# Attention in front of two MLPs: small DMAs, scaling, products with V and weight steps at other steps of the loop

## The chip, the cores and the metric

The kernel runs on one core of a Trainium2 chip. The metric is the device time of one execution in microseconds; the median of three runs of the kernel before is 731.0 us (729.5 to 731.06).

## What is computed

The reference pools neighbouring queries in pairs, does softmax attention, and puts the result through two MLPs:

```python
q_pool = q.reshape(B, H, S // 2, 2, D).mean(axis=3)          # B=2, H=8, S=1152, D=64
scores = np.matmul(q_pool, k.transpose(0, 1, 3, 2)) / np.sqrt(D)
scores = scores - np.max(scores, axis=-1, keepdims=True)
attn = np.exp(scores)
attn = attn / (np.sum(attn, axis=-1, keepdims=True) + 1e-09)
x = np.matmul(attn, v)                                       # -> 1152 tokens x 512
h = x @ w_in;  x = (h * np.tanh(softplus(h))) @ w_out        # 512 -> 2048 -> 512
h = x @ w_in2; y = elu(h) @ w_out2                           # 512 -> 2048 -> 512
```

All arrays that the host hands over are float64 for the MLP weights (the kernel reads them as words of 64 bits) and float32 for the rest.

## The kernel before, in words

**Pairs, units, steps.** Attention takes two heads at a time: 8 pairs `n` of heads, each with 576 pooled queries and 1152 keys. A pair has two units `c`: the first 256 queries and the other 320. A unit has 9 steps `kt`, one for each 128 keys, so a pair has 18 steps and the loop runs over steps `s` from 0 to 143 (then a tail). At each step PE computes the scores of 128 keys with both heads into one PSUM bank pair (`qk`, lines 309 and 311; keys and queries are split into high and low parts, so three products, and a fourth subtracts each query's maximum, which lies in the row tile `top`), and ACT takes the exponential into `pt` (line 317).

**Around this, by unit.** POOL adds up part of the exponentials (`add`, line 330). PE multiplies them with V (`av`, line 382, tile C) and sums them over keys (`total`, line 340, tile T). ACT copies the sums out (`spill`, line 355); they go to DRAM and come back in another layout (lines 357 and 360). DVE inverts them (`invert`, lines 365 and 366); the reciprocals go to DRAM (line 368) and come back broadcast over partitions as `rb` (line 372). DVE multiplies C with `rb` (`scale`, line 406), and ACT and DVE write the high and low part of the tokens that the MLPs read (`token_high`, `token_low`).

**Around this, for a pair ahead.** q, k and V of later pairs are loaded (`load_q`, `load_k`, `load_v`), q is pooled and both are split (`pool_q`, `high_*`, `low_*`). The maximum of each query needs all scores ahead of time: in 14 steps `e` PE computes scores of the next pair with high parts alone (`peak_mm`, tile M, lines 255 and 261, the latter for the 64 queries left over, the rest block) and DVE takes their maxima (`peak`, lines 269 to 273). After `e` = 5 and `e` = 13 `top` negates the maxima (lines 281, 283), sends them to DRAM (line 287) and fetches them back as rows (lines 292, 297).

**Weights.** MLP weights come as float64 words and are turned into a high and a low part in steps: `read` (a DMA, line 99), `rebias` (ACT, 111), `clamp` (POOL, 115), `shift` and `words` (DVE, 120, 125, 126), `high` (ACT, 134), `rest` (DVE, 137). During attention one piece of 512 KB begins in each pair, at step 12; each piece counts its steps (`age`), and the ages decide when its next operation is emitted.

**What sets the order.** There is no planner on the chip: the kernel writes every engine's queue in order. `at(s, e, f)` puts a task into step `s` under a key, and each step emits, in this order: maxima matmuls ("peak"), `qk` and `exp`, products with V and sums ("av"), then "act", "dve", "pool", "sp", then the weight pieces. An engine runs its instructions in the order in which they were emitted, and waits at the first that isn't ready. All DMAs of this part are on SP's queue, and SP too waits at the first DMA whose data isn't ready or whose target isn't free. Scores, maxima scores and sums share one ring of three PSUM tiles (tag S, two banks each); C has two.

Steps below are counted in a pair, so the second unit's step `u0 + 24` is step 33, that is 15 of the next pair:

| task | first unit, before | second unit, before |
|---|---|---|
| `av`, two bursts (5 and 4 of 9) | 11, 15 | 2, 6 |
| `total`; `spill` with both its DMAs | 15; 16 | 6; 7 |
| `invert` with both its DMAs | 2 | 11 |
| `scale`; `token_high`; `token_low` | 6; 7; 9 | 15; 16; 0 |

Maxima of the next pair: steps 5 to 10 and 12 to 17, 0 and 1, each `top` with its DMAs at the step of the last of its maxima. Loads of q and k at step 12, of V at 10. After attention the MLPs run over blocks of 384 tokens (`h_mm`, line 170; `out_mm`, line 617); the scaling of the last pair is done between their first units (`after`).

Of the kernel before, what the change touches and what calls it, by code (L numbers as in the profile page):

```python
# [10 lines left out]
F32 = mybir.dt.float32  # L11
# [10 lines left out]
def tile_pool_attention_mish_elu_mlp(  # L22
# [20 lines left out]
    P = 128  # L43
# [131 lines left out]
    def attention():  # L175
        with ExitStack() as st:
# [102 lines left out]
            def top(n, t0, t1):  # L279
                m, g, row = stat[n], neg[n], tops[n % 2]  # L280
                nc.vector.tensor_reduce(g[:, t0:t1, :], m[:, t0:t1], axis=AX.X, op=ALU.max, negate=True)
                if t1 == NQ:
                    nc.vector.tensor_reduce(g[:, t1, 0:1], m[:, t1, 0:1], axis=AX.X, op=ALU.max, negate=True)
                if t0 == 0:
                    hops[n] = dp.tile([P, NQ + 1, 2], F32, tag="hopm", name="hopm")
                hop, e = hops[n], slice(2 * t0, 2 * t1 + (t1 == NQ))
                nc.sync.dma_start(
                    out=hop.rearrange("p t h -> p (t h)")[:, e], in_=g.rearrange("p t h -> p (t h)")[:, e].bitcast(F32)
                )
# [62 lines left out]
            def spill(n, c):  # L352
                w = cut[c][1] - cut[c][0]
                r = ap.tile([P, 5 * D // 2], F32, tag="sum", name="sum")
                nc.scalar.copy(r[:, :w // 2], sums_.pop((n, c))[:, :w // 2])
                hop = dp.tile([P, w // D], F32, tag=f"hop{c}", name="hop")
                nc.sync.dma_start(out=by_four(hop), in_=r.rearrange("(g p) w -> g p w", p=32)[:, 0, :w // 2])
                pool, bufs = home(n)
                r = tots[n, c] = pool.tile([P, w // D], F32, tag=f"tot{c}", name="tot", bufs=bufs)
                nc.sync.dma_start(out=r, in_=hop)  # L360

            def invert(n, c):
                w = cut[c][1] - cut[c][0]
                r = tots.pop((n, c))
                nc.vector.tensor_scalar(r, r, 1e-9, None, op0=ALU.add)
                nc.vector.reciprocal(r, r)
                hop = dp.tile([P, w // D], F32, tag=f"pop{c}", name="pop")
                nc.sync.dma_start(out=hop, in_=r)
                pool, bufs = home(n)
                rb = rbs[n, c] = pool.tile([P, w], F32, tag=f"rb{c}", name="rb", bufs=bufs)  # L370
                for h in range(2):
                    nc.sync.dma_start(
                        out=rb[half[h]].rearrange("p (z w) -> p z w", z=2),
                        in_=by_four(hop)[2 * h:2 * h + 2].partition_broadcast(D),
                    )
# [47 lines left out]
            last = n_pairs * NS  # L423
            for n in range(n_pairs):
                s0 = n * NS
                if n:
                    at(s0 - 24, "sp", load_q, n)
                    at(s0 - 24, "sp", load_k, n)
# [5 lines left out]
                    at(s0 - 13, "pool", low_q, n, nc.gpsimd)  # L434
                    at(s0 - 11, "pool", low_k, n, nc.gpsimd, slice(0, S // 2))
                    at(s0 - 9, "pool", low_k, n, nc.gpsimd, slice(S // 2, S))
                    at(s0 - 8, "sp", load_v, n)
                    for e in range(6):
                        at(s0 - 13 + e, "peak", peak_mm, n, e)
                        at(s0 - 13 + e, "dve", peak, n, e)  # L440
                    for e in range(6, 14):
                        at(s0 - 6 + e - 6, "peak", peak_mm, n, e)
                        at(s0 - 6 + e - 6, "dve", peak, n, e)
                for c in range(2):
                    u0 = s0 + KT * c
                    for kt in range(KT):
                        at(u0 + kt + 1, "pool", add, n, c, kt)
                        at(u0 + KT + (2 if kt < 5 else 6), "av", av, n, c, kt)
                    t0 = u0 + KT + 6
                    at(t0, "av", total, n, c)  # L450
                    at(t0 + 1, "act", spill, n, c)
                    if n < n_pairs - 1:
                        at(t0 + 5, "dve", invert, n, c)
                        at(t0 + 9, "dve", scale, n, c)
                        at(t0 + 10, "act", token_high, n, c)
                        at(t0 + 12, "dve", token_low, n, c)
                    else:
                        at(t0 + 1, "act", keep, n, c)
                        for u, f in (1 + c, invert), (3 + 3 * c, scale), (3 + 3 * c, token_high), (4 + 3 * c, token_low):
# [26 lines left out]
            low_q(0, nc.gpsimd, c1)  # L486
            for e in range(6, 14):
# [3 lines left out]
                else:  # L491
                    at(e - 10, "peak", peak_mm, 0, e)
                    at(e - 10, "dve", peak, 0, e)
            for s, e in sorted(x for x in todo if x[0] < 0):
# [4 lines left out]
            while s < last or todo or going:  # L499
# [10 lines left out]
                for w in list(going):  # L510
                    w.age += 1
                    if w.age == 4:
                        w.rebias()
                    elif w.age == 5:
                        w.clamp()
                    elif w.age == 7:
                        w.shift()
                    elif w.age == 8:
                        w.words()
                    elif w.age == 9:  # L520
                        w.high()
                    elif w.age == 10:
                        w.rest()
# [238 lines left out]
```

## Time and profile before

| | |
|---|---|
| runs | 731.0 us median (729.5 to 731.06) |
| profiled execution | 730.59 us on the device, span of the instructions 728.8 us |
| mean granted TensorE clock | 0.946 of full |
| busy | PE 668.0 us (92%), DVE 431.4 (59%), ACT 337.8 (46%), POOL 229.6 (32%) |
| DMA | 53.37 MB, 73 GB/s on average |
| attention | to about 316 us; the MLPs fill the rest |

Busy time of PE is that of pipelined matmuls: a matmul's end is modelled, so two in a row can overlap, and a matmul at the lower clock counts as busy for longer. How long a piece of work takes on PE is better read from the starts of successive matmuls. A record "x2" stands for several instructions of the same kind merged into one row.

### The profile page before, as it was taken

To read this page: it belongs to the slowest core of one execution; us is meant where nothing else is said; L and a number is where in the kernel's file an instruction comes from. 1 tells how busy PE (TensorE), PEld (TensorE's weight loads), DVE (VectorE), ACT (ScalarE), POOL (GpSimd) and SP (SyncE) were. 2 spreads that over 40 slices of the span, in tenths; PEclk is the share of its full clock that TensorE was granted. 3 is DMA by queue.
4 is the path that set the end of the run, shared out by engine and by line. 5 is a ranking of instruction groups with operands and counts; after the bars stand their busy time and mean duration, and the time that the engine had idled before them with its cause. 6 is when DMAs were issued, how large, how long until landed. Compare 5 with 4: busy or idle time off the path is not lost.

```text
span 728.8 us, 11613 instructions
## 1 busy us (share of the span) xinstructions
PE 668.0 (92%) x4616; PEld 559.9 (77%) x4616; DVE 431.4 (59%) x700; ACT 337.8 (46%) x680; POOL 229.6 (32%) x213
## 2 busy tenths in 40 slices
PE   4988887888789788979999999999999999999997
PEld 2655555555556555659999999999999999999996
DVE  5555444445454554136745656677698778897453
ACT  2553333435253433444444344444566665675442
POOL 3766364547455263611110123223331101110000
PEclk9999798898969798998999999999999999999999
DMA  3131304040311312133313222222222212320111
GB/s 111 52 127 34 113 9 136 9 137 9 110 36 39 100 23 58 48 95 125 116 58 116 86 62 88 83 87 87 65 80 85 87 61 60 115 87 1 44 44 44
DMA packets 47175, 53.37 MB, mean 73 GB/s; under 512 B 18640, under 2 KB 38032, under 8 KB 47120
## 3 DMA queue, kind: packets, MB, share of 16 engines
q1 hardware_dynamic: 46608, 51.91, 23.3%
q8 instruction: 36, 0.59, 0.3%
q10 hardware_dynamic: 512, 0.72, 0.3%
q14 instruction: 19, 0.16, 0.1%
HBM read 50.14 MB, written 2.47 MB: 72 GB/s over the span
## 4 chain that ended last, share of the span: by engine, by line
PE 54%; DMA 1%; ACT 0%; DVE 0%; issue 0%; SPq 0%
PE A L170 27%; PE B L617 22%; PE C L617 5%; DMA raw<-in_moe_w_out_dram 1%; DVE part L642 0%; DMA hop<-sum 0%; ACT L571 0%; ACT g L572 0%; SPq L99 0%; ACT gh L571 0%; SPq L360 0%; ACT wf L111 0%
## 5 line engine op out<-in xcount | busy, mean ns | idle before, releaser
L317 ACT ACTIVATE pt<-S 128x512 f32<-128x512 f32 (+1 forms) x144 | 91.2, 650 | 171.4 <-PE S L311 170.8
L115 POOL TENSOR_SCALAR wf<-wf 128x512 f32<-128x512 f32 x64 | 44.0, 687 | 308.6 <-ACT wf L111 266.9
L170 PE MATMUL A<-XH,wh 128*128 128x384 f32 x384 | 130.4, 340 | 4.3 <-ACT g L572 3.5
L170 PE MATMUL A<-XL,wh 128*128 128x384 f32 x384 | 130.1, 339 | 0.0
L170 PE MATMUL A<-XH,wl 128*128 128x384 f32 x384 | 130.1, 339 | 0.0
L269 DVE TENSOR_REDUCE stat<-M 128x2 f32<-128x768 f32 x96 | 89.2, 954 | 52.5 <-PE M L255 52.2
L309 PE MATMUL S<-QH,KH 64*128 64x320 f32 (+1 forms) x288 | 58.4, 400 | 34.6 <-DVE stat L269 31.3
L382 PE MATMUL C<-pt,vr 128*64 128x320 f32 (+1 forms) x576 | 88.6, 459 | 0.0
L309 PEld LDWEIGHTS S<-QH,KH 64*128 64x128 f32 x288 | 30.7, 208 | 62.2 <-DVE stat L269 43.0
L170 PEld LDWEIGHTS A<-XH,wh 128*128 128x128 f32 x384 | 72.5, 189 | 6.7 <-ACT g L572 3.8
L170 PEld LDWEIGHTS A<-XL,wh 128*128 128x128 f32 x384 | 72.6, 189 | 1.8
L330 POOL TENSOR_TENSOR add<-pt 128x512 f32<-128x512 f32 (+1 forms) x32 | 45.3, 1414 | 87.1 <-ACT pt L317 87.1
L170 PEld LDWEIGHTS A<-XH,wl 128*128 128x128 f32 x384 | 72.6, 189 | 0.0
L382 PEld LDWEIGHTS C<-pt,vr 128*64 128x64 f32 x576 | 42.9, 152 | 35.2 <-issue 17.2
L330 POOL TENSOR_TENSOR add<-add,pt 128x512 f32<-128x512 f32 (+1 forms) x48 | 69.7, 1473 | 0.0
L137 DVE TENSOR_TENSOR wl<-wf,wh 128x512 fp32r<-128x512 f32 x64 | 49.4, 772 | 25.2 <-ACT wh L134 25.2
L571 ACT ACTIVATE gh<-A 128x384 fp32r<-128x384 f32 x48 | 23.6, 491 | 71.8 <-PE A L170 71.8
L255 PE MATMUL M<-KH,QH 64*128 64x384 f32 x192 | 42.5, 438 | 14.8 <-DVE stat L269 6.2
L111 ACT ACTIVATE wf<-raw 128x512 f32<-128x512 f32 x64 | 43.1, 674 | 21.8 <-DMA raw<-in_moe_w_in_dram 13.7
L126 DVE SCALAR_TENSOR_TENSOR wf<-raw,wf 128x512 int32<-128x512 int32 x64 | 51.8, 809 | 2.2
L617 PE MATMUL B<-gh,wh 128*128 128x384 f32 x155 | 52.3, 338 | 0.0
L617 PE MATMUL B<-gl,wh 128*128 128x384 f32 x155 | 52.3, 337 | 0.0
(90 smaller groups left out, 1312.2 us busy)
## 6 DMA issues: line engine op xcount, KB each, us to landing
raw<-in_moe_w_in_dram SPq DMA_DIRECT2D x32, 512.0 KB
raw<-in_moe_w_out_dram SPq DMA_DIRECT2D x32, 512.0 KB
vr<-in_v_dram SPq DMA_DIRECT2D x8, 576.0 KB
qr<-in_q_dram SPq DMA_DIRECT2D x7, 576.0 KB
kr<-in_k_dram SPq DMA_DIRECT2D x7, 576.0 KB
out_dram<-part SPq DMA_DIRECT2D x8, 256.0 KB
rb<-pop SPq DMA_DIRECT2D x16, 80.0 KB
rb<-pop SPq DMA_DIRECT2D x16, 64.0 KB
```

Of the source, the lines that this page charges most:

```text
L111: nc.scalar.activation(self.f, self.top.bitcast(F32), AF.Identity, scale=2.0 ** -112)
L115: nc.gpsimd.tensor_scalar(self.f, self.f, HUGE, -HUGE, op0=ALU.min, op1=ALU.max)
L126: nc.vector.scalar_tensor_tensor(f, self.low, 29, f, op0=ALU.logical_shift_right, op1=ALU.bitwise_or)
L137: eng.tensor_tensor(self.l, self.f, self.h, op=ALU.subtract)
L170: nc.tensor.matmul(pt[:, :TB], w[:, kk * P:(kk + 1) * P], x[:, kk, tk], start=(i == 0), stop=(i == len(terms) - 1))
L255: nc.tensor.matmul(pt[:, h, :KB], qh[n][half[h], t * P:(t + 1) * P], kh[n][half[h], j * KB:(j + 1) * KB], start=True, stop=True,)
L269: nc.vector.tensor_reduce(m[:, t, :, j], pt[:, :, :KB], axis=AX.X, op=ALU.max)
L309: nc.tensor.matmul(pt[:, h, :w], x[half[h], kk], y[half[h], cols], start=(i == 0), stop=False)
L317: nc.scalar.activation(pts[n, c][:, kt], sc.pop((n, c, kt))[:, :, :w], AF.Exp, scale=SCALE)
L330: nc.gpsimd.tensor_tensor(d, d if i is None else p[:, i], p[:, j], op=ALU.add)
L382: nc.tensor.matmul(acc[n, c][half[h], :w], vs[n][:, h, kt, :], pts[n, c][:, kt, h, :], start=(kt == 0), stop=(kt == KT - 1),)
L617: nc.tensor.matmul(pt, l, r, start=(first and i == 0), stop=(final and i == 2))
```

## The change

Nothing is computed in another way; tasks are emitted at other steps, and the helper functions are cut where a DMA to DRAM and the DMA back stood together (`top` into `top`, `top_out`, `top_in`; `spill` into `spill`, `sum_out`, `sum_in`; `invert` into `invert`, `inv_out`, `inv_in`), so that each is emitted by itself. In steps of a pair, the new places are:

| task | first unit | second unit |
|---|---|---|
| `av`, three bursts of 3 | 11, 14, 17 | 2, 5, 8 |
| `total`; `spill`; `sum_out`; `sum_in` | 14; 15; 16; 0 | 5; 6; 7; 9 |
| `invert`; `inv_out`; `inv_in` | 3; 4; 6 | 12; 13; 15 |
| `scale`; `token_high`; `token_low` | 9; 10; 12 | 0; 1; 3 |

The maxima of the next pair are at steps 4, 6 to 13, 15 to 17, 0 and 1; the first `top_out` at 11 and `top_in` at 13, the second at 2 and 4. q and k are loaded at step 13, V at 14; `low_q` and both halves of `low_k` are at 8, 9 and 10 (before 5, 7 and 9). A weight piece has its operations at ages 4, 6, 8, 9, 10 and 13 (before 4, 5, 7, 8, 9 and 10).

```diff
     def top(n, t0, t1):
-        m, g, row = stat[n], neg[n], tops[n % 2]
+        m, g = stat[n], neg[n]
         nc.vector.tensor_reduce(g[:, t0:t1, :], m[:, t0:t1], axis=AX.X, op=ALU.max, negate=True)
...
             nc.vector.tensor_reduce(g[:, t1, 0:1], m[:, t1, 0:1], axis=AX.X, op=ALU.max, negate=True)
+
+    def top_out(n, t0, t1):
         if t0 == 0:
             hops[n] = dp.tile([P, NQ + 1, 2], F32, tag="hopm", name="hopm")
-        hop, e = hops[n], slice(2 * t0, 2 * t1 + (t1 == NQ))
-        nc.sync.dma_start(
-            out=hop.rearrange("p t h -> p (t h)")[:, e], in_=g.rearrange("p t h -> p (t h)")[:, e].bitcast(F32)
-        )
+        e = slice(2 * t0, 2 * t1 + (t1 == NQ))
+        hop, g = (x.rearrange("p t h -> p (t h)")[:, e] for x in (hops[n], neg[n]))
+        nc.sync.dma_start(out=hop, in_=g.bitcast(F32))
+
+    def top_in(n, t0, t1):
+        hop, row = hops[n], tops[n % 2]
         for h in range(2):
...
     def spill(n, c):
+        w = (cut[c][1] - cut[c][0]) // 2
+        r = tots[n, c] = ap.tile([P, 5 * D // 2], F32, tag="sum", name="sum")
+        nc.scalar.copy(r[:, :w], sums_.pop((n, c))[:, :w])
+
+    def sum_out(n, c):
         w = cut[c][1] - cut[c][0]
-        r = ap.tile([P, 5 * D // 2], F32, tag="sum", name="sum")
-        nc.scalar.copy(r[:, :w // 2], sums_.pop((n, c))[:, :w // 2])
-        hop = dp.tile([P, w // D], F32, tag=f"hop{c}", name="hop")
+        hop = hops[n, c] = dp.tile([P, w // D], F32, tag=f"hop{c}", name="hop")
+        r = tots.pop((n, c))
         nc.sync.dma_start(out=by_four(hop), in_=r.rearrange("(g p) w -> g p w", p=32)[:, 0, :w // 2])
+
+    def sum_in(n, c):
         pool, bufs = home(n)
-        r = tots[n, c] = pool.tile([P, w // D], F32, tag=f"tot{c}", name="tot", bufs=bufs)
-        nc.sync.dma_start(out=r, in_=hop)
+        r = tots[n, c] = pool.tile([P, (cut[c][1] - cut[c][0]) // D], F32, tag=f"tot{c}", name="tot", bufs=bufs)
+        nc.sync.dma_start(out=r, in_=hops.pop((n, c)))
...
     def invert(n, c):
-        w = cut[c][1] - cut[c][0]
-        r = tots.pop((n, c))
+        r = tots[n, c]
         nc.vector.tensor_scalar(r, r, 1e-9, None, op0=ALU.add)
         nc.vector.reciprocal(r, r)
-        hop = dp.tile([P, w // D], F32, tag=f"pop{c}", name="pop")
-        nc.sync.dma_start(out=hop, in_=r)
+
+    def inv_out(n, c):
+        hop = hops[n, c] = dp.tile([P, (cut[c][1] - cut[c][0]) // D], F32, tag=f"pop{c}", name="pop")
+        nc.sync.dma_start(out=hop, in_=tots.pop((n, c)))
+
+    def inv_in(n, c):
+        hop = hops.pop((n, c))
         pool, bufs = home(n)
-        rb = rbs[n, c] = pool.tile([P, w], F32, tag=f"rb{c}", name="rb", bufs=bufs)
+        rb = rbs[n, c] = pool.tile([P, cut[c][1] - cut[c][0]], F32, tag=f"rb{c}", name="rb", bufs=bufs)
         for h in range(2):
...
     last = n_pairs * NS
+    WHEN = [-14, -12, -11, -10, -9, -8, -7, -6, -5, -3, -2, -1, 0, 1]
     for n in range(n_pairs):
...
         if n:
-            at(s0 - 24, "sp", load_q, n)
-            at(s0 - 24, "sp", load_k, n)
+            at(s0 - 23, "sp", load_q, n)
+            at(s0 - 23, "sp", load_k, n)
             at(s0 - 18, "pool", pool_q, n, nc.gpsimd)
...
             at(s0 - 16, "act", blk_q, n)
-            at(s0 - 13, "pool", low_q, n, nc.gpsimd)
-            at(s0 - 11, "pool", low_k, n, nc.gpsimd, slice(0, S // 2))
-            at(s0 - 9, "pool", low_k, n, nc.gpsimd, slice(S // 2, S))
-            at(s0 - 8, "sp", load_v, n)
-            for e in range(6):
-                at(s0 - 13 + e, "peak", peak_mm, n, e)
-                at(s0 - 13 + e, "dve", peak, n, e)
-            for e in range(6, 14):
-                at(s0 - 6 + e - 6, "peak", peak_mm, n, e)
-                at(s0 - 6 + e - 6, "dve", peak, n, e)
+            at(s0 - 10, "pool", low_q, n, nc.gpsimd)
+            at(s0 - 9, "pool", low_k, n, nc.gpsimd, slice(0, S // 2))
+            at(s0 - 8, "pool", low_k, n, nc.gpsimd, slice(S // 2, S))
+            at(s0 - 4, "sp", load_v, n)
+            for e, r in enumerate(WHEN):
+                at(s0 + r, "peak", peak_mm, n, e)
+                at(s0 + r, "dve", peak, n, e)
+            for r, t0, t1 in (WHEN[5], 0, 2), (WHEN[13], 2, NQ):
+                at(s0 + r + 1, "sp", top_out, n, t0, t1)
+                at(s0 + r + 3, "sp", top_in, n, t0, t1)
         for c in range(2):
...
                 at(u0 + kt + 1, "pool", add, n, c, kt)
-                at(u0 + KT + (2 if kt < 5 else 6), "av", av, n, c, kt)
-            t0 = u0 + KT + 6
+                at(u0 + KT + 2 + kt // 3 * 3, "av", av, n, c, kt)
+            t0 = u0 + KT + 5
             at(t0, "av", total, n, c)
             at(t0 + 1, "act", spill, n, c)
+            at(t0 + 2, "sp", sum_out, n, c)
+            at(t0 + 4, "sp", sum_in, n, c)
             if n < n_pairs - 1:
-                at(t0 + 5, "dve", invert, n, c)
-                at(t0 + 9, "dve", scale, n, c)
-                at(t0 + 10, "act", token_high, n, c)
-                at(t0 + 12, "dve", token_low, n, c)
+                at(t0 + 7, "dve", invert, n, c)
+                at(t0 + 8, "sp", inv_out, n, c)
+                at(t0 + 10, "sp", inv_in, n, c)
+                at(t0 + 13, "dve", scale, n, c)
+                at(t0 + 14, "act", token_high, n, c)
+                at(t0 + 16, "dve", token_low, n, c)
             else:
-                at(t0 + 1, "act", keep, n, c)
-                for u, f in (1 + c, invert), (3 + 3 * c, scale), (3 + 3 * c, token_high), (4 + 3 * c, token_low):
+                at(u0 + KT + 9, "act", keep, n, c)
+                u = 3 + 3 * c
+                for u, f in (
+                    (c, invert), (c, inv_out), (1 + c, inv_in), (u, scale), (u, token_high), (u + 1, token_low)
+                ):
                     after.setdefault(u, []).append(lambda f=f, c=c: f(n_pairs - 1, c))
...
     low_q(0, nc.gpsimd, c1)
+    top_out(0, 0, 2)
+    top_in(0, 0, 2)
     for e in range(6, 14):
...
             at(e - 10, "dve", peak, 0, e)
+    at(4, "sp", top_out, 0, 2, NQ)
+    at(5, "sp", top_in, 0, 2, NQ)
     for s, e in sorted(x for x in todo if x[0] < 0):
...
             w.age += 1
-            if w.age == 4:
-                w.rebias()
-            elif w.age == 5:
-                w.clamp()
-            elif w.age == 7:
-                w.shift()
-            elif w.age == 8:
-                w.words()
-            elif w.age == 9:
-                w.high()
-            elif w.age == 10:
-                w.rest()
+            f = {4: w.rebias, 6: w.clamp, 8: w.shift, 9: w.words, 10: w.high, 13: w.rest}.get(w.age)
+            if f:
+                f()
+            if w.age == 13:
                 going.remove(w)
```

## Rows read from the trace of the kernel before

**Rows 1.** The page's slices: granted TensorE clock in tenths, 40 slices of the span.

```profile
PEclk9999798898969798998999999999999999999999
```

**Rows 2.** Stages: length, each engine's busy us (xinstructions), PEclk, DMA share, GB/s.

```profile
190.00:233.00 43.00, 35.53 (x323) 23.34 (x323) 19.76 (x31) 16.79 (x32) 21.78 (x17) 0.84 0.26 73
400.00:728.80 328.80, 324.23 (x1721) 306.28 (x1719) 231.77 (x380) 175.35 (x363) 54.94 (x66) 1.00 0.22 70
```

**Rows 3.** PE's timeline (start, us, line, matmul): rest block's first score matmuls.

```profile
44.34 0.62 PE L261 MATMUL M<-KH,blk 128*128 128x384 f32 x2
...
202.52 1.01 PE L261 MATMUL M<-KH,blk 128*128 128x384 f32 x2
...
243.75 1.01 PE L261 MATMUL M<-KH,blk 128*128 128x384 f32 x2
...
283.13 1.01 PE L261 MATMUL M<-KH,blk 128*128 128x384 f32 x2
```

**Rows 4.** Waits, 25 to 320 us: who waited for what, total us, times, longest.

```profile
DVE y L406 <- DMA rb<-pop: 58.1, 14, 6.6
...
PE S L309 <- DVE stat L269: 31.2, 32, 3.9
```

**Rows 5.** SP's queue, 187 to 202 us: start, issue time in us, line, tiles.

```profile
187.43 1.70 SPq L292 DMA_DIRECT2D top<-hopm  x2
189.18 0.95 SPq L222 DMA_DIRECT2D vr<-in_v_dram  x1
190.22 0.42 SPq L368 DMA_DIRECT2D pop<-tot  x1
194.10 1.15 SPq L372 DMA_DIRECT2D rb<-pop  x2
195.33 0.53 SPq L217 DMA_DIRECT2D qr<-in_q_dram  x1
```

**Rows 6.** DVE's timeline at that place; in brackets the idle time before it.

```profile
197.51 0.49 DVE L406 TENSOR_TENSOR y<-C,rb 128x320 f32<-128x320 f32 x1 [6.64 <-DMA rb<-pop]
```

**Rows 7.** PE's timeline at that place.

```profile
198.93 0.64 PE L309 MATMUL S<-QH,KH 64*128 64x320 f32 x2 [3.88 <-DVE stat L269]
```

**Rows 8.** Stretches of 2 us, columns as in rows 2.

```profile
38.00:40.00 2.00, 2.00 (x22) 1.40 (x22) 0.96 (x1) 1.13 (x2) 2.00 (x2) 1.00 1.05 426
...
200.00:202.00 2.00, 1.52 (x12) 1.07 (x10) 1.28 (x3) 1.31 (x4) 0.00 (x0) 0.50 0.87 306
```

**Rows 9.** PE's timeline in pair 7, which has no score maxima beside it.

```profile
291.18 0.28 PE L309 MATMUL S<-QH,KH 64*128 64x256 f32 x2
...
291.65 0.28 PE L309 MATMUL S<-QH,KH 64*128 64x256 f32 x2
...
292.70 2.37 PE L382 MATMUL C<-pt,vr 128*64 128x320 f32 x16
295.01 0.75 PE L340 MATMUL T<-pt,ones 128*32 128x160 f32 x16
...
296.23 0.39 PE L309 MATMUL S<-QH,KH 64*128 64x256 f32 x2
```

**Rows 10.** PE's timeline: two successive steps of 320 columns with a maximum.

```profile
224.06 0.41 PE L309 MATMUL S<-QH,KH 64*128 64x320 f32 x2 [0.42 <-DVE stat L269]
...
225.26 0.41 PE L309 MATMUL S<-QH,KH 64*128 64x320 f32 x2 [0.17 <-DVE stat L269]
```

**Rows 11.** DVE in one pair, by form; then line 137 (ns min/median/max) before 320 us.

```profile
L269 DVE TENSOR_REDUCE stat<-M 128x2 f32<-128x768 f32 x12 | 11.2, 954 | 8.7 <-PE M L255 8.7
...
L137 DVE TENSOR_TENSOR wl<-wf,wh x8: 691/1226/1367, 53.1 to 314.6; 128x512 fp32r<-128x512 f32 x8
```

**Rows 12.** PE at the MLP's start, and SP's issue of the first weights there.

```profile
316.72 0.45 PE L170 MATMUL A<-XH,wh 128*128 128x384 f32 x1 [0.78 <-ACT x L390]
...
326.75 0.69 PE L170 MATMUL A<-XH,wh 128*128 128x384 f32 x1 [3.51 <-ACT g L572]
...
318.34 0.43 SPq L99 DMA_DIRECT2D raw<-in_moe_w_in_dram  x1
```

## The prediction, made before the changed kernel was run

> **What bounds the kernel now.** I read the slices of the page first. The clock row [rows 1] falls below 9 only in eight of the first 19 of 40 slices, the attention part, and stands at 9 behind it. The table by stage [rows 2] says the same in numbers. From 400 us to the end PE is busy 324.23 of 328.80 us at a clock of 1.00: the MLP part is bound by its own matmuls, and nothing of this change runs there. In 190 to 233 us PE is busy 35.53 of 43 us at a mean clock of 0.84. With only two levels (1.2 and 2.4 GHz) a mean of 0.84 is 0.32 x 43 = 13.8 us at the low one. DVE (19.76), ACT (16.79) and POOL (21.78) are each busy half of the time. So in attention no engine is full, and the one that looks full works at half clock for a third of the time.
>
> How long a pair of heads takes is read from the rest block's score matmuls, which come once a pair at its step 0 [rows 3]: 44.34, ..., 202.52, 243.75, 283.13 us (seven starts), so pairs 1 to 6 take 238.8 us, 39.8 each.
>
> Next come the waits [rows 4]. DVE waited 58.1 us for the broadcast reciprocals (rb), at 14 of the scale steps, 8.3 us a pair; PE waited 31.2 us for DVE to empty a score bank. These are one chain. On SP's queue [rows 5] the reciprocals go out at 190.22 us, behind V's 576 KB. SP then stands until that write has landed, and issues the reload at 194.10, with the loads of q and k queued behind it. DVE, which runs in order, stands at the scale for 6.64 us until 197.51 [rows 6], with score maxima queued behind it. All three score banks are then taken, and PE stands 3.88 us until 198.93 [rows 7]. After that gap the granted clock is 0.50 [rows 8], until PE has been busy without a break again.
>
> **The change, part by part.** It adds and drops no arithmetic and no DMA; all is order. Times are from the profiled execution, 730.59 us on the device with a span of 728.8; the median of the runs shown is 731.0, so the two may be exchanged.
>
> What a pair costs PE at the high clock and without waits, by starts of matmuls in a stretch without score maxima [rows 9]: one QK step of 256 columns 0.47 us, so 0.59 at 320 columns by the ratio of widths. Products with V, 320 wide, 2.31 us for 16 records, so 5.2 for the unit's 36; 256 wide, by that ratio, 4.2. Sums 1.22 and, by width, 1.0. A step of 320 columns with its max matmul has a pitch of 1.20 us, of which 0.17 is a wait for DVE [rows 10], so 1.03 without; at 256 columns 0.91.
>
> The new order on PE by steps of a pair. Bursts of V products (a third of a unit) come at steps 2, 5, 8 (320 wide, 1.73 each) and 11, 14, 17 (256 wide, 1.39 each); sums at 5 and 14; no maxima at 2, 3, 5, 14. Steps 2 and 3: 0.47 + 1.73 and 0.47. Step 5: 0.47 + 1.73 + 1.22 = 3.42. Step 8: 0.91 + 1.73 = 2.64. Steps 11 and 17: 1.03 + 1.39 = 2.42 each. Step 14: 0.59 + 1.39 + 1.0 = 2.98. Together 16.6 us. The eleven steps with a maximum and no burst are 10.6 us without waits (five of 0.91, six of 1.03) and 13.2 at the measured 1.20. So a pair lies between 27.2 and 29.8 us. I take 29.0: five of the eleven follow straight behind a burst, in which DVE catches up (5 x 0.17 to 0.42, about -1.2), and DVE has two scales, a low half and an inversion between maxima (about +0.4). A second way gives the same: the pair that begins at 202.52 us took 41.2 us; without the idle time of PE (about 7) and half of the 14 us at the low clock, both as in rows 2, it would be 27.2, and waits of the size of rows 10 stay.
>
> *Scale, 13 steps behind the sums, and its DMAs apart.* Does rb now come in time? Second unit: inversion at step 12, done by 0.7 us into step 13; then SP issues the reciprocals (0.42), two stabiliser rows (1.7), q and k (0.95), V (0.95) and the reload, at the durations of rows 5. The write takes up to 3.9 us from issue to the reload's issue, so the reload goes out 5.0 us into step 13. Ahead of it are 1.73 MB of q, k and V, issued from 2.9 us on; at the 426 GB/s of rows 8 they take 4.1 us and are done at 7.0. The reload itself took 3.4 us from issue to DVE [rows 5, 6], so it is there between 8.4 and 10.4. DVE comes to the scale after steps 13 to 17 (1.2 + 2.98 + 1.2 + 1.2 + 2.42 = 9.0) and the maximum of the next step (1.2): 10.2. Wait: 0 to 0.2 us, against 6.64 before. First unit: from step 4 SP has the reciprocals, four stabiliser DMAs and the reload, some 5 us, then 3.4; the scale comes at step 9, 9.7 us on, with 1.2 more. No wait. I take 0 for both; the cover is about 1 us deep, and what it costs when it goes is in the third rival.
>
> *Clock.* With the 3 to 4 us gaps gone PE is busy 26 to 27 of 29 us. In rows 7 and 8 the low level follows a gap of 3.88 us; gaps as in rows 10 are not followed by it. I take the high level throughout, bounded by the low level staying (fourth rival).
>
> *Weights over nine steps, lows and loads later.* The second half of the chain on DVE falls on steps 2, 3 and 7; step 3 has no maximum. POOL keeps its 21.8 us, in 29. ACT gets the high halves of q and k and a token cast at step 1, some 2 us, in front of a burst of 1.73. Value 0, bounds -1 to +1 us a pair. In one chain on DVE the rows show what POOL's company costs: `wl` takes 0.69 us at best and 1.23 in the median [rows 11].
>
> The Trainium skill, GPSIMD Engine Reference (Specifications and Key points), says that GpSimd shares its SBUF interfaces with VectorE, and that DVE instructions with two SBUF inputs contend with it. That speaks against this change, since POOL's share of a pair rises from 22 of 40 to 22 of 29. The trace agrees in kind, by the spread of `wl`. By that rule three weight instructions and the low tokens of every pair would take their long times, about 1 us more, and the sum would be 667 instead of 660.
>
> *Sum.* Pairs 1 to 6: 6 x (39.8 - 29.0) = 65 us. Pair 7 has no maxima; it took 33.6 us (283.13 to the MLP's first matmul at 316.72 [rows 12]), with one low stretch: -3. Pair 0, without scales to wait for: -0.5. The end: the sums of the last unit now come ahead of its last burst, so the first MLP weights, at 318.34 behind SP's last small DMAs, go out some 1.7 us sooner against PE; PE's 3.51 us gap before 326.75 waits on the engine that waits for them [rows 12]: -2, bounds 0 and -4. Together -70.5: 730.6 - 70.5 = 660.
>
> **Rivals.** (1) *Every wait of DVE hides behind a burst.* For it: the bursts now stand on both sides of the full stretches. Against it: maxima alone are 12 x 0.954 = 11.2 us of DVE [rows 11], in steps shorter than 1.2. Pair 27.2: 11 us less, 649. (2) *Only the idle time comes back:* the low clock has another cause than the scale's gap. For it: the clock row is below 9 in eight slices spread over attention, and does not tell by itself what PE did ahead of them [rows 1]. A pair gives back 7 less the 2 of rows 10, 5 x 6, and the ends 5: 695. Against it: 0.50 stands right behind the gap. (3) *The wait moves.* Three bulk loads now stand between the two halves of the reciprocals' trip. If rb comes 3 us late, DVE stands, PE with it, and one low stretch of 7 us (3.5 lost) follows in each pair: 29 + 3 + 3.5 = 35.5, so 699. For it: a cover of 1 us, less if the steps are faster. Against it: slower steps give the cover back. (4) *Slower:* the same place, decided by the rate of the bulk loads. DVE's waits of a pair must pass the old 8.3 us; then rb lands 18.5 us into step 13, that is q, k and V take 12 us, 145 GB/s or less. Then a pair is 41 us: 737. Against it stand the 426 and 306 GB/s of rows 8.
>
> **How the numbers follow.** Forecast (650 to 676, pair of 27.5 to 31.5): 0.60, 660 us. Rival 1: 0.15. Rivals 2 and 3: 0.11 and 0.09. Rival 4: 0.04; no change 0.01. The range 643 to 692 takes in the forecast, rival 1 and a share of rivals 2 and 3 that bring less than their full price: about 0.80. Under 0.2% (1.5 us) this kernel's runs can't tell from no change; faster 0.95, same 0.01, slower 0.04.
>
> **What would show it.** Right: seven starts of the rest block's matmuls about 29 us apart; DVE's wait for rb under 10 us in all; clock of attention at 0.97 or more; PE's waits for DVE many, and each under 0.6 us; MLP unchanged at 412 us. Wrong: rb still first among DVE's waits (rivals 3, 4); PE idle time gone and 0.50 still in the windows (rival 2); a new name at the head of PE's waits, POOL's adds before the sums or the stabiliser rows, which now start two steps after their maxima.

## The result, and the profile after

The changed kernel takes 684.35 us, median of four runs, against 730.61 us: a ratio of 0.9361, 95% interval [0.9336, 0.9386]. The forecast was 660 us in a range of 643 to 692. One of the four executions (788.23 us) ran at a mean granted clock of 0.76 from end to end and is left out of the ratio. The profile below is of the same kernel run again (685.07 us median, ratio 0.9377 [0.9315, 0.9439], span of the profiled execution 682.0 us).

The clock row of the page answers to [rows 1]: two slices below 9 where there were eight.

```profile
PEclk9999999989898999999999999999999999999999
```

The stages answer to [rows 2] (same columns). The same 43 us of the span now hold more steps of attention: PE's clock is 0.96, and DVE does 26.38 us of work where it did 19.76. In the MLP part, at clock 1.00, PE is busy 277.42 of 282 us.

```profile
190.00:233.00 43.00, 37.55 (x381) 24.66 (x381) 26.38 (x42) 18.91 (x37) 26.92 (x20) 0.96 0.24 68
400.00:682.00 282.00, 277.42 (x1451) 259.47 (x1449) 202.95 (x336) 154.85 (x319) 43.80 (x53) 1.00 0.21 68
```

The rest block's first matmuls on PE's timeline answer to [rows 3]. From 45.73 to 242.44 us are six pairs, 32.8 us each, against 39.8. Their mean granted clock is 0.97, where it was 0.86 for the six pairs of before.

```profile
45.73 0.62 PE L261 MATMUL M<-KH,blk 128*128 128x384 f32 x2
...
207.96 0.62 PE L261 MATMUL M<-KH,blk 128*128 128x384 f32 x2
...
242.44 0.62 PE L261 MATMUL M<-KH,blk 128*128 128x384 f32 x2
```

The waits from 25 to 320 us answer to [rows 4]. DVE waits 21.7 us for rb where it waited 58.1, in 6 places: five are scales of a second unit (2.7 to 4.2 us), the sixth (5.6 us) stands in pair 7, which has no maxima behind it. PE's waits for the ordinary maxima (L269) have gone from 31.2 us to 7.2, but five waits for the maximum of the rest block (L271), 8.0 us together, are new.

```profile
DVE y L420 <- DMA rb<-pop: 21.7, 6, 5.6
...
PE S L313 <- DVE stat L271: 8.0, 5, 2.5
PE S L313 <- DVE stat L269: 7.2, 21, 0.4
```

Where that comes from is seen on SP's queue at one pair's step 13, which answers to [rows 5]: the reciprocals go out at 198.05 us, then q, k and V, and the reload is issued at 203.04 behind them.

```profile
198.05 0.32 SPq L379 DMA_DIRECT2D pop<-tot  x1
...
200.88 1.16 SPq L217 DMA_DIRECT2D qr<-in_q_dram  x1
...
202.61 0.38 SPq L222 DMA_DIRECT2D vr<-in_v_dram  x1
203.04 2.00 SPq L386 DMA_DIRECT2D rb<-pop  x2
```

DVE's timeline there answers to [rows 6]. It stands 4.17 us at the scale, the longest of the five such waits, and only then takes the rest block's first maximum:

```profile
210.76 0.49 DVE L420 TENSOR_TENSOR y<-C,rb 128x320 f32<-128x320 f32 x1 [4.17 <-DMA rb<-pop]
211.16 0.95 DVE L271 TENSOR_REDUCE stat<-M 128x2 f32<-128x768 f32 x1
```

PE's timeline, as [rows 7]: the rest block's second matmul at 209.18, then 2.54 us without work until that maximum is out of its bank.

```profile
209.18 0.45 PE L261 MATMUL M<-KH,blk 128*128 128x384 f32 x1
212.17 0.39 PE L313 MATMUL S<-QH,KH 64*128 64x256 f32 x2 [2.54 <-DVE stat L271]
```

Stretches of 2 us, as [rows 8]: the three loads move at 368 GB/s, from about 202.5 to 208.5 us. The reload, which is in the queue behind them, lands at 210.7.

```profile
202.00:204.00 2.00, 1.77 (x42) 1.30 (x30) 0.78 (x1) 0.19 (x1) 1.73 (x2) 1.00 0.74 191
204.00:206.00 2.00, 1.62 (x16) 1.18 (x18) 1.46 (x3) 1.21 (x3) 1.35 (x1) 1.00 0.97 368
206.00:208.00 2.00, 2.00 (x21) 1.13 (x19) 0.58 (x1) 1.33 (x3) 1.13 (x2) 1.00 0.97 367
208.00:210.00 2.00, 1.62 (x13) 0.98 (x11) 0.00 (x0) 0.60 (x1) 1.07 (x2) 1.00 0.18 49
```

At the MLP's start, as [rows 12], PE's gap is 1.76 us where it was 3.51; the clock stays at 1.00 behind it, where it was 0.50 from 326 to 330 us before. From 274.00 us to the end are 408 us, 4 fewer than before.

```profile
274.00 0.45 PE L170 MATMUL A<-XH,wh 128*128 128x384 f32 x1 [0.53 <-ACT x L404]
...
282.31 0.44 PE L170 MATMUL A<-XH,wh 128*128 128x384 f32 x1 [1.76 <-ACT g L590]
```

### The profile page after: what moved, and what is told of

It is laid out like the page before. It is cut to its first block, busy times and chain, and to the rows that moved or that the text cites. A ratio compares the mean times of both kernels' runs of the same rounds, so it can differ in the third digit from the quotient of the medians.

```text
span 786.4 us, 11612 instructions
## 1 busy us (share of the span) xinstructions
PE 760.6 (97%) x4616; PEld 591.5 (75%) x4616; DVE 433.6 (55%) x700; ACT 340.4 (43%) x680; POOL 227.3 (29%) x213
## 4 chain that ended last, share of the span: by engine, by line
PE 89%; DVE 5%; DMA 2%; ACT 2%; issue 1%; SPq 0%; POOL 0%; DVEq 0%
PE A L170 31%; PE B L635 25%; PE C L396 11%; PE S L313 8%; PE C L635 6%; DVE stat L269 5%; PE M L255 3%; PE T L344 3%; PE S L315 2%; PE M L261 1%; DMA rb<-pop 1%; ACT pt L321 1%; DMA qr<-in_q_dram 0%; ACT KH L239 0%; DMA top<-hopm 0%
## 5 line engine op out<-in xcount | busy, mean ns | idle before, releaser
L170 PE MATMUL A<-XH,wh 128*128 128x384 f32 x384 | 147.3, 384 | 0.5 <-ACT x L404 0.5
L170 PE MATMUL A<-XH,wl 128*128 128x384 f32 x384 | 147.1, 383 | 0.0
L170 PE MATMUL A<-XL,wh 128*128 128x384 f32 x384 | 147.0, 383 | 0.0
L269 DVE TENSOR_REDUCE stat<-M 128x2 f32<-128x768 f32 x96 | 90.3, 957 | 87.6 <-PE M L255 86.8
L396 PE MATMUL C<-pt,vr 128*64 128x320 f32 (+1 forms) x576 | 100.1, 495 | 0.0
L170 PEld LDWEIGHTS A<-XL,wh 128*128 128x128 f32 x384 | 75.5, 197 | 10.2
L592 DVE TENSOR_TENSOR gl<-g,gh 128x384 fp32r<-128x384 f32 x48 | 29.6, 616 | 63.2 <-ACT g L590 63.2
L635 PE MATMUL B<-gl,wh 128*128 128x384 f32 x155 | 59.7, 385 | 0.0
L635 PE MATMUL B<-gh,wh 128*128 128x384 f32 x155 | 59.6, 385 | 0.0
L635 PE MATMUL B<-gh,wl 128*128 128x384 f32 x155 | 59.6, 385 | 0.0
L607 DVE SCALAR_TENSOR_TENSOR e<-e,r 128x384 f32<-128x384 f32 x48 | 26.7, 556 | 53.6 <-ACT r L605 53.5
L635 PE MATMUL B<-wh,gh 128*128 128x512 f32 x117 | 53.5, 457 | 0.0
```

What stands on the lines that cost most here:

```text
L170: nc.tensor.matmul(pt[:, :TB], w[:, kk * P:(kk + 1) * P], x[:, kk, tk], start=(i == 0), stop=(i == len(terms) - 1))
L269: nc.vector.tensor_reduce(m[:, t, :, j], pt[:, :, :KB], axis=AX.X, op=ALU.max)
L396: nc.tensor.matmul(acc[n, c][half[h], :w], vs[n][:, h, kt, :], pts[n, c][:, kt, h, :], start=(kt == 0), stop=(kt == KT - 1),)
L592: nc.vector.tensor_tensor(gl, g, gh, op=ALU.subtract)
L607: nc.vector.scalar_tensor_tensor(e, e, 1.0, t, op0=ALU.add, op1=ALU.mult)
L635: nc.tensor.matmul(pt, l, r, start=(first and i == 0), stop=(final and i == 2))
```

## The experiments

Every run is timed beside the kernel before on the same chip, and its ratio is to those runs. The edits are shown abridged: one `at` can stand for several. Theory A is the prediction's: the distance between sums and scale was too short, so DVE waited, PE stood and lost its clock. Theory B credits the spread bursts of V. Theories C to E came up on the way.

**Profile of the changed kernel again, and one part alone or undone**

> The changed kernel once more, for a profile at the usual clock. Theory A (DVE's wait for the reciprocals set both the gaps and the low clock): DVE's wait for rb under 20 us in all, mean clock 0.98 or more, 684 us, pairs of about 32 us where 29 was forecast, and the missing 3 us a pair found as many short waits of PE for DVE's maxima. Theory B (spreading the products with V does the work): the wait for rb is still near 58 us, and the gain stands in the steps with bursts.

The lines above are of this run. The wait for rb is 21.7 us (A said under 20) and the pair 32.8 us (A said about 32), and B's 58 us is far off. But the missing time isn't in many short waits alone: beside 7.2 us in 21 short waits of score matmuls there are 8.0 us in five long ones behind the scale.

```diff
 # only_scale: kernel before, and
+at(t0 + 2, "sp", sum_out)   +at(t0 + 4, "sp", sum_in)    +at(t0 + 7, "dve", invert)
+at(t0 + 8, "sp", inv_out)   +at(t0 + 10, "sp", inv_in)   +at(t0 + 13, "dve", scale)
```

> The kernel before with one part of the change: the sums', reciprocals' and scale's tasks are emitted at the new distances from the sums (2, 4, 7, 8, 10, 13); bursts of V, maxima, stabiliser rows, loads and weight steps stay as before. Theory A: most of the gain is here, 690 to 705 us, rb's wait under 20 us, few low-clock stretches. Theory B: under 8 us of gain, 723 to 731.

713.28 us, ratio 0.9762 [0.9688, 0.9837]: a gain of 1.6 to 3.1%, in neither range. The wait for rb did go (4.7 us are left), and yet PE's waits for maxima are 19.7 us of the old 31.2. In DVE's waits a new one stands in its place, at the inversion:

```profile
DVE tot L374 <- DMA tot<-hop: 40.2, 13, 5.1
...
PE S L313 <- DVE stat L269: 19.7, 18, 3.8
```

SP's queue at one of these places points to the reason. V (142.91), q, k and a weight piece go out first, then the reciprocals at 145.00, and the reload can be issued only at 152.47, 7.5 us later, where it was 3.9 [rows 5]. While SP stands there, the next unit's sums can't go out (they leave at 153.96).

```profile
142.91 0.42 SPq L222 DMA_DIRECT2D vr<-in_v_dram  x1
...
145.00 0.38 SPq L379 DMA_DIRECT2D pop<-tot  x1
152.47 1.15 SPq L386 DMA_DIRECT2D rb<-pop  x2
```

So distance is not enough. The next runs ask whether it is what stands ahead of a small DMA on the queue that counts.

```diff
 # undo_scale: changed kernel, and the steps of before for this part
-at(t0 + 2, "sp", sum_out) -at(t0 + 4, "sp", sum_in) -at(t0 + 7, "dve", invert) ... -at(t0 + 13, "dve", scale)
+at(t0 + 1, "act", sum_out, sum_in)   +at(t0 + 6, "dve", invert, inv_out, inv_in)   +at(t0 + 10, "dve", scale)
```

> The changed kernel with that one part undone: sums and reciprocals with both their DMAs at one step and the scale at the steps of before; three bursts of V, new places of maxima, loads and weight steps stay. Theory A: most of the gain is lost, 712 to 728 us, rb's wait above 40 us and the low clock back. Theory B: 684 to 695.

678.21 us (676.76 to 679.32), ratio 0.9295 [0.9247, 0.9343], where the changed kernel beside it has 685.07 (679.64 to 686.65). Both theories miss: undoing the part that the prediction credited makes the kernel no slower, and by these runs 1% faster. The second unit's reciprocals then leave at step 11, ahead of q, k (13) and V (14). DVE still waits 24.1 us for rb, in 14 places of at most 3.8 us: the sum of DVE's waits is not what PE loses.

```diff
 # undo_av: changed kernel, and
-at(u0 + KT + 2 + kt // 3 * 3, "av", av)         -t0 = u0 + KT + 5
+at(u0 + KT + (2 if kt < 5 else 6), "av", av)    +t0 = u0 + KT + 6
```

> The changed kernel with two bursts of V a unit and the sums a step later, as before; all else as changed (the scale stays 13 steps behind the sums, so a step later too). Theory A: little, 684 to 694, since PE does the same work and only the catching up of DVE behind bursts is lost (0.3 us at six steps of a pair at most). Theory B: 715 to 728.

666.65 us, ratio 0.9139 [0.9091, 0.9188]: 18 us faster than the change, and with `two_bursts_v_behind` below the fastest kernel. A's range is missed too, on the good side, and B falls. The clock is 0.999, the pairs take 29.8 us. Several things are mixed in it: the bursts, the sums with their DMAs a step later, and the scale a step later; `scale_later` below moves the scale alone.

**What stands ahead of the reciprocals**

```diff
 # only_v_later: kernel before, and
-at(s0 - 8, "sp", load_v, n)
+at(s0 - 4, "sp", load_v, n)
```

> The kernel before with one number changed: V of the next pair is loaded at step 14 of a pair instead of step 10, so it no longer goes out just ahead of the second unit's reciprocals (step 11). Theory C (what counts is which bulk loads stand ahead of the reciprocals on SP's queue, not how far the scale stands behind the sums): the second unit's wait for rb falls from 5.6 us to 2 to 3, most low-clock stretches go, 690 to 708 us. Theory A (the distance of the scale): under 4 us of gain.

710.06 us, ratio 0.9702 [0.9666, 0.9738]. One number gives 20.6 of the change's 46 us, and A gave it under 4. But the time lies just outside C's range, and the second unit's wait for rb is 3.8 us a time (26.5 over 7), not 2 to 3. All of DVE's waits for rb are still 49.3 us of 58.1. What fell is the time at the low clock: the six pairs take 220.0 us at a mean clock of 0.92, before 238.8 us at 0.86, so some 32 us less of it (an estimate from these means), worth up to 16 us. On DVE's timeline the inversion (L375) ends at 176.6 us and the scale starts at 187.43:

```profile
176.45 0.19 DVE L375 RECIPROCAL tot<-tot 128x5 f32<-128x5 f32 x1
...
187.43 0.49 DVE L420 TENSOR_TENSOR y<-C,rb 128x320 f32<-128x320 f32 x1 [5.03 <-DMA rb<-pop]
```

SP's queue in between: the stabiliser's rows (the negated maxima) go out at 176.24, SP stands until they have landed (179.20), issues their reload, and only at 180.97 the reciprocals. So V was one part of what stood ahead, and the stabiliser's round trip is another.

```profile
176.24 0.33 SPq L290 DMA_DIRECT2D hopm<-neg  x1
179.20 1.71 SPq L296 DMA_DIRECT2D top<-hopm  x2
180.97 1.00 SPq L379 DMA_DIRECT2D pop<-tot  x1
183.88 1.14 SPq L386 DMA_DIRECT2D rb<-pop  x2
```

```diff
 # scale_later: changed kernel, and
-at(t0 + 13, "dve", scale)   -at(t0 + 14, "act", token_high)   -at(t0 + 16, "dve", token_low)
+at(t0 + 14, "dve", scale)   +at(t0 + 15, "act", token_high)   +at(t0 + 17, "dve", token_low)
```

> The changed kernel, three bursts of V kept, with the scale and both token splits one step later, so that the second unit's scale comes behind the rest block's first maximum. Theory C: the wait for rb falls by a step's length and no maximum stands behind it, 666 to 674 us, as with two bursts. Theory D (three bursts cost time in themselves, by their switches between score and V matmuls): 681 to 686.

673.95 us, ratio 0.9219 [0.9194, 0.9244], just inside C's range, clock 1.00; D's range is missed, though three bursts may still cost something (below). DVE's timeline: the rest block's maximum (L271) is out before the scale, which waits 0.36 us.

```profile
170.59 0.96 DVE L271 TENSOR_REDUCE stat<-M 128x2 f32<-128x768 f32 x1 [2.01 <-PE M L261]
171.91 0.49 DVE L420 TENSOR_TENSOR y<-C,rb 128x320 f32<-128x320 f32 x1 [0.36 <-DMA rb<-pop]
```

```diff
 # v_behind_reload: changed kernel, and
-at(s0 - 4, "sp", load_v, n)
+at(s0 - 2, "sp", load_v, n)
```

> The changed kernel with V loaded at step 16 instead of 14, behind the second unit's reload of the reciprocals (step 15); q and k stay ahead of it. Theory C: the reload lands 576 KB earlier, about 1.4 us, so the wait of 4.2 us at the second unit's scale falls to about 2.8, 675 to 681 us. Theory D: no change, 683 to 687.

674.73 us, ratio 0.9225 [0.9201, 0.9249], 0.3 us better than C's range. The wait behaves as C said: at the place of the 4.17 us it is 2.87, and the other four fall from 2.7 to 3.1 us to 1.5 to 1.8. A third of the load ahead of the reload is worth 10 us.

```diff
 # undo_peaks: changed kernel, and
-WHEN = [-14, -12, -11, ...]    top_out, top_in, low_q, low_k, load_q, load_k, load_v as changed
+WHEN = [-13, ..., -8, -6, ...] and all of them at the steps of before
```

> The changed kernel with the places of maxima, stabiliser rows, low parts and of the loads of q, k and V as before; scale, DMAs of sums and reciprocals, bursts and weight steps as changed. Theory C: the second unit's reciprocals (step 13) again go out behind V, q, k and the weights, as in the run with the scale alone, where they took 7.5 us from issue to the reload: 700 to 716 us. Theory A: 684 to 692, as the distance of the scale stays.

698.69 us, ratio 0.956 [0.953, 0.959], 1.3 us under C's range; A's 684 to 692 is missed. The second unit's reciprocals again take 6.6 to 7.6 us from issue to the reload's issue in four of the pairs, as C says.

**That part alone, and how far SP's order alone goes**

```diff
 # only_peaks: kernel before, and WHEN, top_out, top_in, low_q, low_k, load_q, load_k, load_v as changed
```

> The kernel before with one part of the change: the new places of the maxima, of the stabiliser rows, of the low parts and of the loads of q, k and V. Scale, sums, reciprocals, bursts of V and weight steps stay as before, so the second unit's reciprocals (step 11) go out ahead of q, k (13) and V (14). Theory C (the place of the bulk loads on SP's queue): this part alone gives most of the gain, 672 to 690 us, though no scale is moved. Theory A (the distance of the scale): 715 to 728.

684.57 us, ratio 0.9365 [0.9309, 0.9422], in C's range: this part alone gives as much as the whole change. rb's wait is 16.4 us, with the scale at its old distance.

```diff
 # undo_weights: changed kernel, and
-{4: w.rebias, 6: w.clamp, 8: w.shift, 9: w.words, 10: w.high, 13: w.rest}
+{4: w.rebias, 5: w.clamp, 7: w.shift, 8: w.words, 9: w.high, 10: w.rest}
```

> The changed kernel with the weight steps at their old ages (4, 5, 7, 8, 9, 10). Both theories: 682 to 688, nothing that can be told apart. If the old ages are better, since POOL and DVE then do the weights in the steps without maxima, under 680; if the spread was worth something, over 690.

684.47 us, ratio 0.9376 [0.932, 0.9433]: it can't be told from the changed kernel.

```diff
 # two_bursts_v_behind: undo_av, and
-at(s0 - 4, "sp", load_v, n)
+at(s0 - 1, "sp", load_v, n)
```

> The fastest so far (two bursts, sums and scale a step later, all else as changed) with V loaded at step 17, behind the second unit's reload of the reciprocals (step 16). Theory C: the reciprocals wait behind q and k alone, rb's wait falls from 13.0 us to under 6, 660 to 665 us. If q and k alone hold them up: 665 to 668, no change from 666.7.

667.85 us, ratio 0.9145 [0.9082, 0.9208], rb's wait 12.8 us: no change from `undo_av`. A miss for C: what V's place gave with three bursts it doesn't give here, where the scale comes late enough. Of the 12.8 us 10.2 stand in pair 7, and 2.6 in the pairs that have maxima, so there was little left to win.

```diff
 # only_sp_order: kernel before, and
-at(s0 - 8, "sp", load_v, n)                   -top_out, top_in at s0 + r, "dve"
+at(s0 - 4, "sp", load_v, n)                   +at(s0 + r + 1, "sp", top_out)   +at(s0 + r + 3, "sp", top_in)
```

> The kernel before with SP's queue alone put in another order: the stabiliser rows go out one step behind their maxima and come back two steps later, V is loaded at step 14. PE's, DVE's, ACT's and POOL's instructions and their order are those of before; no scale, maximum, burst, low part or weight step is moved. Theory C (what stands ahead of the reciprocals on SP's queue, V's load and the stabiliser's round trip, is the whole cause): as much as all the new places of maxima and loads together, 680 to 692 us, rb's wait under 25 us. Theory E (V's place is half of it, and the other half is that the maxima are spread over more steps): 700 to 710, as with V alone.

696.14 us, ratio 0.951 [0.9476, 0.9544], between C and E, so both miss. No instruction of PE, DVE, ACT or POOL is moved, and 36 us are won, where the whole change wins 46. The inversion ends at 171.36 us on DVE, the reciprocals leave at 171.39 on SP, their reload is issued at 173.99, and the scale waits 0.22 us:

```profile
171.17 0.19 DVE L375 RECIPROCAL tot<-tot 128x5 f32<-128x5 f32 x1
...
177.29 0.49 DVE L420 TENSOR_TENSOR y<-C,rb 128x320 f32<-128x320 f32 x1 [0.22 <-DMA rb<-pop]
```

```profile
171.39 0.33 SPq L379 DMA_DIRECT2D pop<-tot  x1
173.99 1.13 SPq L386 DMA_DIRECT2D rb<-pop  x2
175.17 0.58 SPq L290 DMA_DIRECT2D hopm<-neg  x1
```

rb's wait is 10.6 us in all, against 58.1; DVE also waits 13.2 us at the inversion.

```profile
DVE tot L374 <- DMA tot<-hop: 13.2, 9, 3.9
...
DVE y L420 <- DMA rb<-pop: 10.6, 9, 4.8
```

## Why the prediction was right, and where it was wrong

**What held.** The direction and the range held, and so did the chain that the prediction read at the second unit's scale: the wait for rb, PE's gap behind it and the low clock behind the gap went together. In `scale_later` the scale waits 1.1 us at most in the pairs that have maxima (7.9 of its 10.0 us of rb stand in pair 7), and the clock is 1.00. That speaks against rival 2 at these gaps. The prediction's second way of counting holds for the best kernel: 41.2 us without idle time and low clock plus small waits gave 29.0, and `undo_av` has 29.8. Much of the gain is the clock: the six pairs are 42 us shorter, and by their mean clocks (0.86 in 238.8 us, 0.97 in 196.7) some 55 us less are spent at the low level of 1.2 GHz. By this estimate up to 27 of the 42 us come from the clock.

The range was met at its slow end. Of the signs that the prediction named for being right, the clock of attention came (0.97); pairs of 29 us (32.8), rb under 10 us (21.7) and no wait of PE over 0.6 us (2.5) did not. The range held because it took in a rival 3 at less than its full price, and that is part of what came.

**Which part did it.** The sum booked the gain on the scale 13 steps behind the sums. By the runs, that part alone gives 17 us (713.28), and undone it costs nothing (678.21 against 685.07). The places of the maxima, of the stabiliser's DMAs and of the loads give all of it alone (684.57): 20.6 us V's place, 13.9 more the stabiliser's round trip (696.14), and 11.6 more the rest, that is q and k a step later, the low parts and the maxima over other steps. These are steps of one order of adding the parts, and no run parted the rest. The prediction had named V ahead of the reciprocals in [rows 5] and then priced only the distance; and it had q, k and V between the two halves of the trip as a small matter of cover.

**A second chain that the prediction took for the first.** It read PE's 31.2 us of waits for maxima and DVE's wait for rb as one chain. The trace of the kernel before shows two. Six gaps of PE (18 us) stand behind the second unit's scale, as the prediction says. Six others, 1.2 us each, stand behind `wl`, the last step of a weight piece (line 137), which DVE runs just ahead of the pair's first maximum. One of them:

```profile
213.03 1.22 DVE L137 TENSOR_TENSOR wl<-wf,wh 128x512 fp32r<-128x512 f32 x1 [4.05 <-ACT wh L134]
214.18 0.94 DVE L269 TENSOR_REDUCE stat<-M 128x2 f32<-128x768 f32 x1
...
215.18 0.38 PE L309 MATMUL S<-QH,KH 64*128 64x256 f32 x2 [1.18 <-DVE stat L269]
```

The scale comes only afterwards (216.10), so rb can't be the cause. Behind five of these six gaps the granted clock falls to 0.50 to 0.53 as well (0.50 from 216 to 218 us). For this share of the low clock rival 2 was right. Moving DMAs alone leaves these gaps standing: `only_sp_order` has all six (1.0 to 1.2 us), five of them again with the clock at 0.50 to 0.52 behind them, though its scales then wait 0.9 us at most:

```profile
157.63 1.22 DVE L137 TENSOR_TENSOR wl<-wf,wh 128x512 fp32r<-128x512 f32 x1 [1.77 <-ACT wh L134]
158.78 0.94 DVE L269 TENSOR_REDUCE stat<-M 128x2 f32<-128x768 f32 x1
...
159.78 0.38 PE L313 MATMUL S<-QH,KH 64*128 64x256 f32 x2 [1.19 <-DVE stat L269]
```

In `only_peaks` the first maximum is a step earlier and goes ahead of `wl`, and the gap is gone in five of the six pairs (in the other one, other weight steps stand ahead of the maximum, and PE waits 2.8 us):

```profile
152.33 0.96 DVE L269 TENSOR_REDUCE stat<-M 128x2 f32<-128x768 f32 x1 [0.65 <-PE M L255]
153.43 1.23 DVE L137 TENSOR_TENSOR wl<-wf,wh 128x512 fp32r<-128x512 f32 x1
```

This is the likely body of the 11.6 us: the mean clock of the six pairs is 0.95 in `only_sp_order` and 0.98 in `only_peaks`. No run moved the first maximum or `wl` alone, so the share is argued from traces and not measured. The forecast's "high level throughout" needed this move, and the prediction didn't see that it did.

**The step that failed** is "I take 0 for both; the cover is about 1 us deep". For the first unit 0 came true in pairs 1 to 6; for the second it did not. The issue times came out as worked: in the pair shown the reload goes out 4.9 us into step 13 (198.17 to 203.04), forecast 5.0. The landing did not: 12.6 us, forecast 8.4 to 10.4. The three loads were done at about 10.3 us instead of 7.0, as they started moving late and at 368 GB/s instead of 426, and the reload landed 2.2 us behind them. And DVE did not reach the scale at 10.2 but at 8.4: the rest block's maximum, which the sum put ahead of the scale, is emitted after it in the same step. So a wait of 4.2 us stands where 0 to 0.2 did (2.7 to 3.1 in the other four pairs), with score banks blocked behind it. That is rival 3 at a fraction of its price: PE's gaps behind it are 1.1 to 2.5 us, and the low clock follows in three of the five pairs. `scale_later`, which moves only the scale and the token splits by a step, brings the pair from 32.8 to 31.3 us.

**The term with the wrong sign** is the catching up of DVE behind bursts, -1.2 us a pair. `scale_later` and `undo_av` have the scale at the same step; one has three bursts a unit, the other two, and the sums with the DMAs behind them a step later. A pair of each, columns as in [rows 2], first `scale_later`, then `undo_av`:

```profile
138.59:169.93 31.34, 28.26 (x309) 18.84 (x308) 18.63 (x30) 15.55 (x30) 20.55 (x16) 1.00 0.30 84
```

```profile
133.42:163.02 29.60, 27.72 (x309) 19.05 (x308) 18.35 (x31) 15.65 (x30) 20.66 (x16) 1.00 0.31 89
```

Over the six pairs the means are 31.3 and 29.8 us (one pair of `undo_av` took 30.6): 0.4 us more PE time and 1.0 us more idle time, at the same clock. PE's timeline of `scale_later` behind a burst shows one way in which a burst costs time: the scores of one maximum and one score step run at once, the scores of the second maximum follow, and then PE waits 0.29 us, since DVE had stood idle for 1.51 us at the end of the burst and begins with the first maximum only at 154.93.

```profile
154.45 0.45 PE L255 MATMUL M<-KH,QH 64*128 64x384 f32 x2
...
155.32 0.34 PE L255 MATMUL M<-KH,QH 64*128 64x384 f32 x2
155.95 0.42 PE L313 MATMUL S<-QH,KH 64*128 64x320 f32 x2 [0.29 <-DVE stat L269]
```

So here a burst does not let DVE catch up; it lets DVE run dry, and PE waits at the new start. That explains a part only: two waits of 0.37 us in the same pair, one for the scale and one for an exponential, aren't in the pair of `undo_av` either. In kernel times the two runs are 673.95 and 666.65 us, intervals [0.9194, 0.9244] and [0.9091, 0.9188]. The sums' step is in that difference too, and no run took it out.

**The sum, term by term.** Pairs 1 to 6: 42 us (forecast 65). Of the 3.8 us that a pair takes more than the 29.0, 1.5 is the scale's place, 1.5 the bursts and the sums' step together, and 0.8 stays. (The eleven steps of the sum without waits come to 10.7 us, not 10.6, which changes nothing.) Pair 7: 242.44 to 274.00, 31.6 us, so -2.0 (forecast -3). Before pair 1: +1.4 (forecast -0.5). The MLP: -4 (forecast -2, bounds 0 and -4), with its gap halved and the low clock behind it gone. Weights: nothing, as taken, in the run with the old weight steps. Rival 1 (649 us) did not come: PE is still idle 2.0 us a pair in `undo_av`. Rival 4 did not come either.

What the rule on the shared interfaces (the Trainium skill, GPSIMD Engine Reference, Key points) would add was not seen in a kernel time. In the pairs with maxima `wl` took 1.2 us in the kernel before and with the old weight steps, and 0.68 us in the changed kernel; yet the run with the old weight steps can't be told from the change.

## What to carry to other kernels

On a queue that issues its DMAs in order, ask of every small DMA on a critical round trip what stands ahead of it, both bulk loads and other DMAs that wait for a landing: putting one load behind it was worth 20 us here. Moving the consumer further away gave 17 us alone, and much of its wait came back at the next consumer on the same queue. Where two tasks fall into the same step, look up which is emitted first. Where many gaps carry the same releaser's name, look at each kind of gap by itself: here one kind stood behind the scale and another behind a weight step. Three bursts a unit were not better than two here, against what the prediction had assumed; how much of the difference is the bursts' own was not shown.

## What the runs showed of the hardware

A 2.5 KB write could be reloaded 2.6 us after its issue with nothing ahead (171.39 to 173.99), and 7.5 us after it behind four loads issued 0.6 to 2.1 us earlier (145.00 to 152.47). Three loads of 576 KB issued within 2 us moved at 368 GB/s once under way, and not at the 426 of [rows 8]. In attention the granted clock went to 0.50 in three stretches of the changed kernel, behind gaps of PE of 1.4, 1.5 and 2.5 us, and not behind two others of 1.1 and 1.5 us. In the kernel before it did so behind five of six gaps of 1.2 us. In `scale_later`, where no wait of PE between 25 us and the end of attention is over 0.81 us, it did not.
